# Score tiles without a clearing pass: the first unit on a tile multiplies with all keys of a block

## The chip, the cores and the metric

The kernel runs on one core of a Trainium2 chip. The metric is device time in microseconds of one execution; a kernel's time is the median over several executions. TensorE (PE in the profile, with PEld for its weight loads), VectorE (DVE), ScalarE (ACT), GpSimd (POOL) and SyncE (SP, which only issues DMAs here) each work through their own queue in order and wait for each other by semaphores.

## The reference

Sliding-window causal attention with a distance bias, followed by a feed-forward layer with the activation h * tanh(softplus(h)) (Mish). All inputs and outputs are float32.

```python
# attention: q, k, v are (8, 8, 576, 64); window = 128
scores = q @ k.T / 8 + slopes * (-abs(i - j))
mask = (i - j >= 0) & (i - j < 128)
attn = softmax(where(mask, scores, -1e9))          # / (sum + 1e-9)
x = (attn @ v).transpose(0, 2, 1, 3).reshape(4608, 512)
# feed-forward: w_in (512, 2048), w_out (2048, 512)
h = x @ w_in
out = (h * tanh(softplus(h))) @ w_out
```

## The kernel before

**Chunks and stages.** A chunk is the first 512 rows of one batch; the last 64 rows of all eight batches form a ninth chunk. The feed-forward layer works by chunk. Each float32 operand is split into a high and a low part, and a product is three matmuls (high x high, high x low, low x high). The program has a stage "first" (attention of batch 0, splitting of the weights, first layer of chunk 0) and stages 0 to 4. A stage holds the second layer of the chunks whose first layer is done (the step `second` in stages 0 and 1, `call` of `second_chain` in 2 and 3, of `second_fast` in 4), beside it the attention of the next chunks, and at its end the first layer of a pair of chunks as seven products (`product`), which share sums between the two chunks.

**A unit of attention.** `unit(b, p, half)` does two blocks of 128 queries for the two heads of pair p. Its steps are `scores` (PE), `peak` (VectorE: puts the older keys' scores over the newer block's where the window asks for it, adds the bias, takes the row's extreme), `exps` (ScalarE), `sums` (VectorE), `scale` (POOL), `weights` (PE transposes, then a VectorE product with the masks), `values` (PE), `split_hi` and `split_lo`. `last_unit` does the same for the 64 last rows.

**The score tile.** A score tile (`s`) is two PSUM banks: two heads, and per head two blocks of 256 columns, the older 128 keys and the newer 128. Two such buffers exist and take turns between score tiles, the products of the first layer (`h`, `m`) and others. Each half has a tile of its own, kept for all units of batch 0, and then for all units of a pair of chunks (1 and 2, 3 and 4, and so on). Queries 0 to 63 of a block need only keys 0 to 191 of the 256, queries 64 to 127 only keys 64 to 255; the first block of a batch has no older keys. So a call multiplies 64 queries with 192 keys (128 in the first block). The step `peak` reads the whole block with `copy_predicated`, also the corners that no call writes. Therefore `clear(b, half)` allocates the tile and writes zeros into the corners, two VectorE instructions per tile, ahead of the first unit; later units find finite numbers there.

**What sets the order.** Every step has a nominal time; `in_order` sorts a stage's steps by it, after the table `MOVED` has replaced some of the times by hand. Each engine executes its instructions in the order in which the sorted steps issue them. `idle` steps are filler matmuls in the stage "first" that write an unused tile. The steps carry no line of their own in the profile, since all instructions are issued by one helper (L82); tiles tell them apart: `s<-qk` are scores, `s<-ident,pz` transposes, `po` and `po_c` the second layer, `h` and `m` the first, `gs` and `gc` its split inputs, `pt_0l` last-row tiles, `so` and `si` split weights, `st` streamed weights.

Of the kernel before, what the change touches and what calls it, by code (L numbers as in the profile page):

```python
# [8 lines left out]
F32 = mybir.dt.float32  # L9
# [7 lines left out]
P = 128  # L17
# [1 line left out]

MOVED = {  # L20
    'first': {
# [7 lines left out]
    },  # L29
# [7 lines left out]
    },  # L37
# [9 lines left out]
    },  # L47
# [8 lines left out]
    },  # L56
# [6 lines left out]
    },  # L63
}

# [24 lines left out]
def attention_mish_mlp(  # L90
# [18 lines left out]
    H, D = 2 * NP, P // 2  # L109
# [17 lines left out]
    ps = ctx.enter_context(tc.tile_pool(name="ps", bufs=1, space=bass.MemoryType.PSUM))  # L127

    pe, dve, act, pool, sp = [
        InOrder(tc, e) for e in (nc.tensor, nc.vector, nc.scalar, nc.gpsimd, nc.sync)  # L130
    ]
# [109 lines left out]
    score = {}  # L241
    HEAD = [slice(i * D, (i + 1) * D) for i in range(2)]

    def clear(b, half):
        t = score[(b + 1) // 2, half] = ps.tile([P, 2, 512], F32, tag="s", name=f"s{b}_{half}", bufs=2)
        v = t.rearrange("p i (c u n) -> p (i c) u n", u=2, n=P)
        v = v if half else v[:, 1::2]
        dve.memset(v[HEAD[0], :, 1, D:], 0.0)
        dve.memset(v[HEAD[1], :, 0, :D], 0.0)

    def unit(b, p, half, turn=(0, 0), give=(0, 0), total=(0, 0), low=0, when=(0.9, 1.98, 2.04)):


# [6 lines left out]
        name = f"{b}_{p}_{half}"  # L260

        def scores():
            qk = qkv[(b, p)]
            key = ((b + 1) // 2, half)
            t = score[key]
            st["s"] = [t[:, i, :] for i in range(2)]
            st["all"] = t.rearrange("p i (c u n) -> p (i c) u n", u=2, n=P)
            q0 = 0 if half == 0 else 832
            for a, j in enumerate(blocks):
                for h in range(2):  # L270
                    k0, k1 = (D * h, D * h + 192) if j else (P, 2 * P)
                    for i in range(2):
                        pe.matmul(
                            st["s"][i][HEAD[h], 256 * a + k0 : 256 * a + k1],
                            lhsT=qk[HEAD[i], q0 + a * P + D * h : q0 + a * P + D * h + D],
                            rhs=qk[HEAD[i], 128 + j * P + k0 : 128 + j * P + k1], start=True, stop=True,
                            skip_group_check=True,
                        )
# [89 lines left out]
        t = half  # L368
# [84 lines left out]
    def loads(b, p):  # L453
        nxt = (b, p + 2) if p + 2 < NP else (b + 1, p + 2 - NP)
        if 0 < nxt[0] < B:
            return [lambda: load_qk(*nxt), lambda: load_v(*nxt)]
        return []

    def attention0():
        steps = [(-2 + 0.1 * h, lambda h=h: clear(0, h)) for h in range(2)]  # L460
        for p in range(NP):
            units = [(2 * p, unit(0, p, 0)), (2 * p, last_unit(0, p)), (2 * p + 1, unit(0, p, 1))]
            steps += [(k + d, f) for k, u in units for d, f in u]
            steps += [(2 * p + d, f) for d, f in zip((1.03, 3.01), loads(0, p))]
        return steps

    def attention(b, starts, form):

        steps = [(0.05 + 0.01 * h, lambda h=h: clear(b, h)) for h in range(2) if b % 2]
        for p in range(NP):
            k = starts[p]
            for u in (unit(b, p, 0, *form), last_unit(b, p, *form), unit(b, p, 1, *form)):
                steps += [(k + d, f) for d, f in u]
            steps += [(k + d, f) for d, f in zip((4.9, form[1][1] + 0.06), loads(b, p))]
        return steps
# [100 lines left out]
    steps = [(START + UNIT * t, f) for t, f in attention0()]  # L579
# [21 lines left out]
    for j in range(NJ):  # L601
        t = X0 + SLOT * j
# [500 lines left out]
    for s in range(len(PAIRS) + 1):  # L1103
# [7 lines left out]
        for o, c in enumerate(chunks):  # L1111
# [4 lines left out]
            for m in range(2 * NJ):  # L1116
# [4 lines left out]
                if s == 0 and m >= 2:  # L1121
                    t = PARTS[m - 2]
# [15 lines left out]
        if s < len(PAIRS):  # L1138
            a, b = PAIRS[s]
# [19 lines left out]
            for n in range(3):  # L1159
                t = (20, 30, 33) if s == 0 else (L - 7.5, L - 1.9, L + 0.1) if s >= FAST else (L - 7.5, L - 6.5, L - 5.5)  # L1160
# [13 lines left out]
            for k in range(len(PROD)):  # L1174
                n = 1 if s == 0 and k < 2 else 2
                for i in range(0, NF // 2, n):
# [4 lines left out]
                    for m in range((1, 2, 1, 2, 2, 3, 2)[k]):  # L1181
                        t = L + 8 * k + i + n + (0, 0.6, 2.5)[m] * (1 if m else 0)
                        if s == 0 and k < 2:
                            t = (t - 0.4, L + 24.6 + 0.8 * i)[m]
                        if m == 1 and k in (3, 5):
                            t = L + 8 * k + i + n + 0.1
                        put(t, lambda k=k, i=i, m=m: post[(k, i)][m][1]())
            nxt = split_fast if s + 1 == LAST else split_chain if s + 1 >= FAST else parts
            for n in range(2 if nxt is parts else 3):
                t = (51, 53) if nxt is parts else (50.7, 52.1, 53.2)  # L1190
# [96 lines left out]
```

## Time and profile before

| | us |
|---|---|
| median of 3 runs | 930.28 (927.7 to 930.71) |
| the profiled execution's own time | 927.47 |
| its span, first to last instruction | 925.8 |
| PE busy | 903.6 |
| VectorE busy | 654.0 |
| ScalarE busy | 469.3 |
| POOL busy | 430.5 |

Busy time is the union of an engine's instructions. Matmul ends are modelled, so a busy PE need not be at its peak. The stages of the profiled execution begin at about 88 us (stage 0), 254 (1), 458 (2), 661 (3) and 843 (4).

### The profile page before, as it was taken

To read this page: it belongs to the slowest core of one execution; us is meant where nothing else is said; L and a number is where in the kernel's file an instruction comes from. 1 tells how busy PE (TensorE), PEld (TensorE's weight loads), DVE (VectorE), ACT (ScalarE), POOL (GpSimd) and SP (SyncE) were. 2 spreads that over 40 slices of the span, in tenths; PEclk is the share of its full clock that TensorE was granted. 3 is DMA by queue.
4 is the path that set the end of the run, shared out by engine and by line. 5 is a ranking of instruction groups with operands and counts; after the bars stand their busy time and mean duration, and the time that the engine had idled before them with its cause. 6 is when DMAs were issued, how large, how long until landed. Compare 5 with 4: busy or idle time off the path is not lost.

```text
span 925.8 us, 17172 instructions
## 1 busy us (share of the span) xinstructions
PE 903.6 (98%) x6353; PEld 751.6 (81%) x6353; DVE 654.0 (71%) x1509; ACT 469.3 (51%) x1074; POOL 430.5 (47%) x316
## 2 busy tenths in 40 slices
PE   7998999999999999999999999999999999999998
PEld 3586777778778787888788999888799998888897
DVE  6989787685566677446688897545698645457986
ACT  5785655544464454352455646343555543336443
POOL 3202588714678877104667675014567670241000
PEclk9999999999999999999999999999999999999999
DMA  9999436798224444785426734855535367553823
GB/s 369 425 421 423 179 133 219 262 345 277 91 104 151 151 164 168 255 275 203 165 98 208 258 137 161 263 194 191 188 108 177 136 214 243 189 182 137 295 95 111
DMA packets 68291, 193.66 MB, mean 209 GB/s; under 512 B 10608, under 2 KB 14320, under 8 KB 64880
## 3 DMA queue, kind: packets, MB, share of 16 engines
q1 hardware_dynamic: 66544, 191.39, 58.2%
q10 hardware_dynamic: 1664, 1.18, 0.4%
q8 instruction: 50, 0.82, 0.4%
q14 instruction: 33, 0.27, 0.1%
HBM read 153.75 MB, written 38.80 MB: 208 GB/s over the span
## 4 chain that ended last, share of the span: by engine, by line
PE 80%; DVE 11%; ACT 4%; DMA 2%; POOL 2%; issue 2%; DVEq 0%; SPq 0%; POOLq 0%; ACTq 0%
PE m L82 31%; PE po L82 14%; PE po_c L82 13%; PE po_f L82 9%; PE s L82 6%; PE o L82 5%; DMA st<-wcS 2%; DVE to L82 2%; DVE pz L82 1%; ACT pz L82 1%; DVE ti L82 1%; POOL gc L82 1%; POOL pz L82 1%; DVE s L82 1%; DVE sm L82 1%
## 5 line engine op out<-in xcount | busy, mean ns | idle before, releaser
L82 PE MATMUL m<-xT,st 128*128 128x512 f32 x768 | 175.8, 389 | 0.4 <-DMA st<-wcS 0.4
L82 PEld LDWEIGHTS m<-xT,st 128*128 128x128 f32 x768 | 144.0, 188 | 30.9 <-issue 1.1
L82 PE MATMUL po<-so,gs 128*128 128x512 f32 x576 | 141.0, 398 | 0.0
L82 PE MATMUL m<-x,st 128*128 128x512 f32 x576 | 134.4, 391 | 0.0
L82 PEld LDWEIGHTS po<-so,gs 128*128 128x128 f32 x576 | 106.1, 189 | 25.8 <-issue 4.6
L82 PEld LDWEIGHTS m<-x,st 128*128 128x128 f32 x576 | 107.4, 188 | 23.2 <-ACT A L82 0.5
L82 ACT ACTIVATE pz<-pz,mx 128x128 f32<-128x128 f32 x256 | 99.5, 390 | 27.1 <-DVE mx L82 24.9
L82 POOL TENSOR_TENSOR D<-A,C 128x1024 f32<-128x1024 f32 x16 | 39.1, 2451 | 148.9 <-DVE A L82 84.6
L82 POOL TENSOR_TENSOR pz<-pz,sm 128x512 f32<-128x512 f32 x64 | 71.1, 1112 | 73.2 <-DVE sm L82 33.3
L82 PE MATMUL po_c<-so,gc 128*128 128x256 f32 x768 | 102.5, 289 | 1.8 <-POOL gc L82 1.8
L82 PEld LDWEIGHTS po_c<-so,gc 128*128 128x128 f32 x768 | 95.3, 192 | 7.4 <-issue 3.1
L82 DVE TENSOR_TENSOR pz<-s,masks 128x1024 f32<-128x1024 f32 x56 | 66.6, 1215 | 14.8 <-PE s L82 13.3
L82 PE MATMUL po_c<-sf,gc 128*128 128x256 f32 x576 | 73.4, 285 | 0.0
L82 PEld LDWEIGHTS po_c<-sf,gc 128*128 128x128 f32 x576 | 70.4, 191 | 1.7 <-issue 0.8
L82 DVE TENSOR_TENSOR A<-m,A 128x1024 f32<-128x1024 f32 x32 | 39.2, 1224 | 34.4 <-PE m L82 34.4
L82 POOL TENSOR_TENSOR C<-A,C 128x1024 f32<-128x1024 f32 x16 | 39.9, 2494 | 48.0 <-DVE A L82 36.2
L82 DVE CUSTOM_DVE_ANT_0 pz<-s,nb 128x128 f32<-128x128 f32 x256 | 59.2, 287 | 3.6
L82 PE MATMUL s<-qk 64*64 64x192 f32 (+1 forms) x1024 | 49.4, 324 | 10.3 <-DVE s L82 8.8
L82 DVE COPY_PREDICATED s<-older,s 128x256 f32<-128x256 uint16 x64 | 35.6, 556 | 25.7 <-PE s L82 25.5
L82 POOL TENSOR_TENSOR gc<-D,gc 128x512 fp32r<-128x512 f32 x28 | 39.1, 1415 | 28.8 <-ACT gc L82 26.6
L82 PEld LDWEIGHTS s<-qk 64*64 64x64 f32 x1024 | 32.8, 135 | 24.1 <-issue 18.1
L82 PE MATMUL o<-pz,va 128*64 128x128 f32 (+1 forms) x560 | 52.0, 320 | 0.0
(207 smaller groups left out, 1620.5 us busy)
## 6 DMA issues: line engine op xcount, KB each, us to landing
sf<-wdT SPq DMA_DIRECT2D x72, 512.0 KB, 4.5
st<-wcS SPq DMA_DIRECT2D x64, 512.0 KB, 4.7
st<-wr SPq DMA_DIRECT2D x48, 512.0 KB, 5.6
qk<-in_qk_dram SPq DMA_DIRECT2D x31, 640.0 KB, 5.9
va<-in_v_dram SPq DMA_DIRECT2D x28, 320.0 KB, 3.4
wi<-in_moe_w_in_dram SPq DMA_DIRECT2D x8, 1024.0 KB, 14.0
wo<-in_moe_w_out_dram SPq DMA_DIRECT2D x8, 1024.0 KB, 19.6
wr<-si SPq DMA_DIRECT2D x8, 1024.0 KB, 15.3
```

Source lines behind the costliest of these rows:

```text
L82: ins = method(*args, **kwargs)
```

## The change

The function `clear` and its steps go. The first unit on each tile (pair 0 of batch 0 and of chunks 1, 3, 5 and 7) allocates the tile in its own `scores` step and multiplies its queries with all 256 keys of a block, except in the first block of a batch, which still has 128. The other units are as before.

```diff
-    def clear(b, half):
-        t = score[(b + 1) // 2, half] = ps.tile([P, 2, 512], F32, tag="s", name=f"s{b}_{half}", bufs=2)
-        v = t.rearrange("p i (c u n) -> p (i c) u n", u=2, n=P)
-        v = v if half else v[:, 1::2]
-        dve.memset(v[HEAD[0], :, 1, D:], 0.0)
-        dve.memset(v[HEAD[1], :, 0, :D], 0.0)
...
             qk = qkv[(b, p)]
-            key = ((b + 1) // 2, half)
-            t = score[key]
+            full = p == 0 and (b == 0 or b % 2)
+            if full:
+                score[half] = ps.tile([P, 2, 512], F32, tag="s", name=f"s{b}_{half}", bufs=2)
+            t = score[half]
...
-                    k0, k1 = (D * h, D * h + 192) if j else (P, 2 * P)
+                    k0, k1 = (P, 2 * P) if not j else (0, 2 * P) if full else (D * h, D * h + 192)
...
-        steps = [(-2 + 0.1 * h, lambda h=h: clear(0, h)) for h in range(2)]
+        steps = []
...
-        steps = [(0.05 + 0.01 * h, lambda h=h: clear(b, h)) for h in range(2) if b % 2]
+        steps = []
```

The table `MOVED` is new for the stage "first" and stages 0 to 3 (the numbers of the steps shift by two where the clears were). On PE the steps at the start of each stage come in this order, with half 0 and half 1 for the scores of the first unit and "last" for those of the last rows:

```
stage 0 before: second(0,0), last, [clears] half 0, second(1,0), half 1, second(0,1), second(1,1)
stage 0 after:  half 0, second(0,0), second(0,1), half 1, last, second(1,0), second(1,1)
stage 1 before: last, [clears] half 0, half 1, second(0,0), second(0,1)
stage 1 after:  second(0,0), half 0, half 1, last, second(0,1)
stage 2 before: [clears] half 0, call 0, half 1, call 1, call 2, last
stage 2 after:  half 0, call 0, half 1, last, call 1, call 2
stage 3 before: [clears] half 0, call 0, call 1, half 1, last, call 2
stage 3 after:  half 0, call 0, half 1, call 1, call 2, last
```

Here second(j, t) is six matmuls with weight block j for row block t. In the stage "first" some 15 of 54 PE steps change place, `idle` fillers among them; after the first unit's scores six fillers now come ahead of the half-1 scores. Within stages 0, 1 and 3 `second` or `call` steps change places with transposes (`weights`) and `values`, last-row steps with main ones. On VectorE a few `weights`, last-row and split steps swap, in the stage "first" the words of weight block 2 come ahead of the low part of block 1; on ScalarE about eight steps move; on POOL two pairs swap; on SP the store of last rows with a load, and some stores of weight sums.

## Rows read from the trace of the kernel before

**Rows 1.** The page: busy us (share) of each engine, and the chain's shares.
```profile
PE 903.6 (98%) x6353; PEld 751.6 (81%) x6353; DVE 654.0 (71%) x1509; ACT 469.3 (51%) x1074; POOL 430.5 (47%) x316
...
PE 80%; DVE 11%; ACT 4%; DMA 2%; POOL 2%; issue 2%; DVEq 0%; SPq 0%; POOLq 0%; ACTq 0%
```

**Rows 2.** Waits of PE, whole span: who for whom, us, times, longest.
```profile
PE s L82 <- DVE s L82: 8.8, 4, 3.5
PE s L82 <- POOL pz L82: 2.8, 4, 1.5
PE po_c L82 <- POOL gc L82: 1.8, 6, 0.5
...
PE m L82 <- DMA st<-wcS: 0.4, 1, 0.4
```

**Rows 3.** Timeline at the start of stage 0: start us, us, engine, instruction [idle before].
```profile
83.16 1.01 ACT L82 ACTIVATE g<-h 128x1024 f32<-128x1024 f32 x1
...
85.68 1.52 PE L82 MATMUL po<-so,gs 128*128 128x512 f32 x6
...
87.38 1.01 ACT L82 ACTIVATE g<-h 128x1024 f32<-128x1024 f32 x1
88.16 2.43 DVE L82 TENSOR_TENSOR so<-to,so 128x1024 fp32r<-128x1024 f32 x2
...
90.61 1.22 DVE L82 MEMSET s<- 64x128 f32 x4
...
91.19 0.78 PE L82 MATMUL s<-qk 64*64 64x128 f32 x16 [3.51 <-DVE s L82]
...
92.02 0.43 DVE L82 COPY_PREDICATED s<-older,s 128x256 f32<-128x256 uint16 x1 [0.19 <-PE s L82]
...
92.94 1.28 ACT L82 ACT_TABLE_LOAD   x1 [3.08 <-DVE mx L82]
...
94.04 1.56 PE L82 MATMUL s<-qk 64*64 64x192 f32 x16
94.23 0.40 ACT L82 ACTIVATE pz<-pz,mx 128x128 f32<-128x128 f32 x1
...
97.86 1.04 POOL L82 TENSOR_TENSOR pz<-pz,sm 128x512 f32<-128x512 f32 x1 [6.14 <-DVE pt_0l L82]
...
100.05 0.60 PE L82 MATMUL s<-ident,pz 128*128 128x128 f32 x4
```

**Rows 4.** Windows: stretch, length, busy PE, PEld, DVE, ACT, POOL, clock, DMA, GB/s.
```profile
91.00:97.00 6.00, 5.81 (x43) 3.76 (x44) 3.25 (x18) 3.15 (x10) 0.71 (x1) 0.72 1.02 417
460.00:466.00 6.00, 5.75 (x53) 4.62 (x54) 2.92 (x16) 3.10 (x6) 1.28 (x1) 0.72 0.84 334
660.00:668.00 8.00, 6.08 (x65) 4.65 (x64) 4.55 (x16) 3.53 (x5) 2.87 (x3) 1.00 0.73 263
5.00:42.00 37.00, 31.69 (x322) 17.91 (x320) 32.14 (x127) 26.13 (x88) 10.69 (x12) 1.00 1.02 422
42.00:85.00 43.00, 43.00 (x189) 35.21 (x188) 39.34 (x38) 32.14 (x33) 3.73 (x2) 1.00 1.02 423
```

**Rows 5.** Timelines at the starts of stages 1, 2 and 3.
```profile
251.18 1.22 DVE L82 TENSOR_TENSOR A<-A,m 128x1024 f32<-128x1024 f32 x1 [1.50 <-PE m L82]
253.90 1.22 DVE L82 TENSOR_TENSOR A<-A,m 128x1024 f32<-128x1024 f32 x1 [1.50 <-PE m L82]
...
255.71 1.67 PE L82 MATMUL s<-qk 64*64 64x128 f32 x32 [1.45 <-DVE s L82]
...
458.43 1.22 DVE L82 TENSOR_TENSOR A<-A,m 128x1024 f32<-128x1024 f32 x1 [1.50 <-PE m L82]
...
460.25 0.77 PE L82 MATMUL s<-qk 64*64 64x128 f32 x16 [1.93 <-DVE s L82]
...
662.77 0.78 PE L82 MATMUL s<-qk 64*64 64x128 f32 x16 [1.92 <-DVE s L82]
...
666.53 0.88 PE L82 MATMUL s<-qk 64*64 64x192 f32 x16
```

68 rows, old and new, of the table MOVED are left out of this document.

## The prediction

> **What bounds the kernel now.** I read the page's busy shares first, then the chain that ended last: TensorE (PE) is busy for 903.6 of 925.8 us and carries 80% of the chain [rows 1]. So only what makes PE wait, or makes it slower, is worth anything, and the next view is who PE waited for [rows 2]. One entry stands out: four waits of 8.8 us in total, longest 3.5 us, of a score multiplication (`s`) on VectorE (DVE) work on the same score tile. PE and DVE meet on `s` in that direction at the clears, and there are four starts of stages 0 to 3 where a pair of tiles is cleared. I then went to each of the four in the order of time.
>
> At the first, near 88 us, PE has little to do from the end of its six `po` matmuls (85.68 + 1.52 = 87.2) until 91.19; VectorE is in the two subtractions `so` from 88.16 and reaches the clears only at 90.61 [rows 3]. The tile itself was free much earlier: its former content `h` was read at 83.16 to 84.17. So the wait is not for the tile but for a VectorE queue in which the clear stands last. The other three look alike: the last `A` operation (at 253.90, and at 458.43 for stage 2) reads the *other* score buffer; the buffer that the first unit gets was read by the `A` before it (251.18 + 1.22 = 252.4); and the clears stand behind the last one. PE idles 1.45, 1.93 and 1.92 us [rows 5].
>
> The windows add a second cost. From 91 to 97 us and from 460 to 466 us the granted clock averages 0.72 of full speed, so 0.28 x 6 = 1.7 us of full-speed work is lost in each, right behind the idle 3.51 and 1.93 us [rows 4]. The fourth, with 1.92 us, shows 1.00 from 660 to 668. The 16 matmuls of a half-1 unit tell the same: 1.56 us at 94.04, 0.88 at 666.53 [rows 3, 5].
>
> **The change part by part.**
>
> *Wider first units, five times (batch 0 and chunks 1, 3, 5, 7).* Per unit every call is two instructions. A half-0 unit has 8 instructions with 128 columns and 8 with 192 (0.78 us, at 662.77), a half-1 unit 16 with 192 (0.88 us, at 666.53) [rows 5]. So 64 columns more on 8 instructions cost 0.10 us. The change widens 8 instructions of half 0 and 16 of half 1: 0.30 us of PE per start. The wide shape is in no row; from below the cost is 0 (hidden in an idle PE, as for batch 0, where PE waits anyway), from above it is 0.6 us, if such a unit runs at half clock. I take 0.30 at four starts, 0 at batch 0. On this the Trainium skill, "TensorEngine Tiling", section "Tiling Modes", says that the 64x64 mode has four independent tiles. The rows don't bear that out: 8 x 64 = 512 columns in 0.10 us is about two columns at a time at 2.4 GHz, not four. By that section of the Trainium skill the cost would be an estimated 0.15 us per start and the time 0.6 us lower.
>
> *Twenty clears go.* Four take 1.22 us of VectorE per start [rows 3]; what it is worth is the waits. I also have to say what is late next, since the new order changes what PE does there.
>
> *Start of stage 0.* New PE order: half-0 scores, two `second` steps of 6 matmuls, half-1 scores, last scores, three more `second` steps, then the transposes of the first weights. PE is free for them at 85.7 [rows 3]. Half 0 takes 0.88, so 86.6; two steps at 1.52 or a little less each (row at 85.68) 89.6; half 1 needs the last `h` read at 87.38 + 1.01 = 88.4, is not held, and ends at 90.7; the last-row scores are smaller than a half-0 unit, under 0.78; three steps, 96.0 at the latest. The other side starts from VectorE, still in `so` until 90.6. It begins `peak` there and not at 92.02, so 1.4 us earlier; the table load follows 0.92 us behind (92.94 - 92.02), at 91.5; the exponentials 1.29 us later, at 92.8; four at 0.40, 94.4; sums of 0.4 us; GpSimd's scale of 1.04 us; transposes at about 96.0. Before, they began at 100.05 [rows 3]. PE waits there for 0 to 1.5 us, and 4.0 us are won: 3.5 of idle and 1.7 of clock, less 0.3 for the columns and what the new wait takes. What waits behind the head of PE's queue, if a score step is held, is all `second` steps, and behind those the slots for the next `gs`.
>
> *Start of stage 1.* The new order puts one `second` step ahead of the scores, and its operands were ready. Idle 1.45 less 0.30: 1.15 us.
> *Start of stage 2.* Same order as before, with the scores at the head; their buffer was left by the `A` before the last, as at 251.18. 1.93 + 1.7 of clock - 0.3 = 3.3 us.
> *Start of stage 3.* Half-1 scores move ahead of the second `call`; the other buffer is free when the last `A` ends, 0.6 us ahead of the old scores (459.65 against 460.25 at stage 2), so at about 662.2, before PE gets there. 1.92 - 0.30 = 1.6 us.
> Bounds of these four together: 0 from below, if each wait finds another name; from above 8.8 + 3.4 - 1.2 = 11.0.
>
> *The refit of stage "first".* About 15 PE steps move, fillers (`idle`) among them. From 42 to 85 us PE is busy 43.00 of 43.00 us, so whatever is won or lost before 42 reaches the boundary. From 5 to 42 VectorE is busy 32.14 of 37 us [rows 4], so at most 4.9 us can be won; I see moves both ways (second-half scores of pair 1 earlier; the last-row `peak` and a split placed ahead of half-1 work, later), and the split of weight block 1 now stands behind 1.9 us of block 2's words. I take 0.3 won, bounds 2 lost and 4.9 won.
>
> *Other moves.* Elsewhere `second` steps swap with transposes, and last-row steps with main ones. On POOL two pairs swap, on SP an `xs` store with a load and some stores of weight sums. No PE wait hangs on these: all PE waits on POOL work are 4.6 us, on DMA `st` 0.4 [rows 2]. I take 0, bounds 2 either way.
>
> *What is late next.* PE comes to later steps 4 to 10 us earlier than its partners were used to. Most of these follow PE, but not all; I take off 0.8, bounds 0 and 4.3.
>
> **Sum.** 4.0 + 1.15 + 3.3 + 1.6 + 0.3 - 0.8 = 9.55 us. The profiled execution took 927.47 us (1.67 of it outside its span), so 917.9, say 918. The median of the three runs is 930.28, 2.8 us above that execution. As a start of 1.93 us idle lost its clock and one of 1.92 did not, I read the 2.8 as one or two more such losses of 1.7; without idle they go too. Against the median I therefore forecast 12 us less.
>
> **The rivals.**
> *The first gain is given back.* At 207 us PE waits 0.4 us for `st`, loaded behind the combined weights that POOL and the DMAs make [rows 2]. If that chain does not follow PE, the 4.0 us (and the 0.3) end there as a wait for `st`: 922.2. For it: it is already the last to arrive. Against: 0.4 us only, and POOL idles in between.
> *The wait changes its name.* If the first unit's buffer is the one read last, PE waits for that reader. Stage 0: scores at 88.4 rather than 91.19, with the idle and clock loss kept, so some 1 us won; stage 1 is covered by the step put ahead, 1.15; at stages 2 and 3 `A` ends at 459.65 against 460.25, 0.6 - 0.3 each. About 2.8 won: 924.7. Against: two buffers take turns, and 83.16 and 251.18 are the reads of the other one.
> *The refit wins more.* PE's waits on POOL (4.6 us) and half of stage first's idle VectorE (2.4) go in part: 3.5 us beyond the forecast, 914.4.
> *Slower: the clock falls in stage first.* From 5 to 42 us PE's 31.69 busy us [rows 4] hold fillers that keep it occupied between waits of up to 1.5 us, and the refit moves them. At half clock that work takes 31.7 us more against 5.3 of idle: up to 26 us lost, and with 9.3 won elsewhere some 944. It decides once about 15 of the 31.7 us run at half. Against: the row's clock is 1.00 with the same number of fillers.
>
> **How the numbers follow.** Forecast 0.57; first gain given back 0.18; the refit wins more 0.12; the wait renamed 0.08; slower by the clock 0.03; no net effect for several small reasons 0.02. The forecast's own range is 915.5 to 921. From 914 to 923 the range takes in the first three and their spread, about 0.82. A measurement can tell about 0.3%, 2.8 us: faster than 927.5 are the first four, 0.93 with their tails off; 0.04 within, 0.03 slower.
>
> **What would show it.** No row of PE waiting on DVE for `s` at stage starts; granted clock 1.00 at 91 to 97 and 460 to 466; score units of 0.88 and 1.08 us in first units; transposes of chunk 1's first unit near 96; the product stage of chunk 2 beginning about 9 us earlier by 843. It is wrong if PE has a wait of over 3 us near 207, if the products of stage first start later than 41.7, or if PE idles at the four starts under another name.

## The result and the profile after

The kernel after takes 919.6 us in the median (919.28 to 920.5, 4 runs) against 930.42 for the kernel before on the same chip (927.7 to 930.71, 4 runs): a ratio of 0.9892 [0.9872, 0.9912]. The profiled executions compare 919.29 with 927.47, that is 8.2 us less; 918.0 (914 to 923) was forecast.

The waits of PE over the whole span (who for whom, us, times, longest), which answer to [rows 2]:

```profile
PE s L84 <- POOL pz L84: 3.5, 4, 1.4
PE po_c L84 <- POOL gc L84: 1.5, 6, 0.4
PE idle L84 <- DVE busy L84: 1.3, 1, 1.3
PE pt_2l L84 <- DVE pz_2l L84: 1.0, 1, 1.0
PE pt_1l L84 <- DVE pz_1l L84: 0.8, 1, 0.8
PE pt_3l L84 <- DVE pf_3l L84: 0.8, 1, 0.8
PE pt_0l L84 <- DVE pz_0l L84: 0.7, 1, 0.7
PE o L84 <- DVE pf L84: 0.7, 1, 0.7
PE m L84 <- DMA st<-wcS: 0.7, 1, 0.7
```

The entry of 8.8 us, `s` on VectorE's `s`, is gone. What is new stands lower down: PE's last-row transposes (`pt_1l`, `pt_2l`) wait for VectorE's last-row scale (`pz_1l`, `pz_2l`), and `st` has grown from 0.4 to 0.7. The windows answer to [rows 4]; the third and fourth hold the starts of stages 2 and 3, which now come earlier:

```profile
5.00:42.00 37.00, 31.75 (x324) 18.14 (x321) 32.48 (x126) 26.12 (x88) 10.99 (x12) 1.00 1.02 422
91.00:97.00 6.00, 5.33 (x28) 4.08 (x25) 3.97 (x28) 5.50 (x20) 2.32 (x3) 1.00 1.01 412
455.00:461.00 6.00, 6.00 (x66) 4.69 (x66) 4.72 (x20) 4.49 (x11) 1.45 (x2) 1.00 0.85 307
650.00:660.00 10.00, 10.00 (x79) 7.84 (x78) 7.25 (x22) 7.45 (x12) 5.46 (x4) 1.00 0.66 240
```

The clock (last but two) is 1.00 in all of them, and PE is busy throughout the starts of stages 2 and 3. The timeline at the start of stage 0 answers to [rows 3]:

```profile
85.86 0.88 PE L84 MATMUL s<-qk 64*64 64x128 f32 x16
86.67 3.01 PE L84 MATMUL po<-so,gs 128*128 128x512 f32 x12
...
88.22 2.44 DVE L84 TENSOR_TENSOR so<-to,so 128x1024 fp32r<-128x1024 f32 x2
89.61 1.09 PE L84 MATMUL s<-qk 64*64 64x256 f32 x16
90.58 0.42 DVE L84 COPY_PREDICATED s<-older,s 128x256 f32<-128x256 uint16 x1
...
91.49 1.28 ACT L84 ACT_TABLE_LOAD   x1 [1.57 <-DVE mx L84]
...
95.08 1.04 POOL L84 TENSOR_TENSOR pz<-pz,sm 128x512 f32<-128x512 f32 x1 [3.27 <-DVE pt_0l L84]
...
96.17 0.66 PE L84 MATMUL s<-ident,pz 128*128 128x128 f32 x4 [0.67 <-POOL pz L84]
...
98.08 1.27 DVE L84 TENSOR_SCALAR pz_0l<-pz_0l,sm_0l 128x128 f32<-128x128 f32 x1
...
99.40 0.33 PE L84 MATMUL pt_0l<-ident,pz_0l 128*128 128x128 f32 x1 [0.74 <-DVE pz_0l L84]
```

Scores run while VectorE is still in the two `so` subtractions; the peak begins when these end (90.58 instead of 92.02), and the transposes start at 96.17 instead of 100.05, 3.9 us earlier. The last two rows show the price: VectorE's last-row scale comes behind a mask product, and PE waits 0.74 us for it (0.61 before, at 103.09).

**Where the time went.** The same matmul of both profiles, start after minus start before, followed through the span:

| at | behind or ahead, us | change in the stretch | forecast |
|---|---|---|---|
| first VectorE peak (5.16 before, 5.52 after) | +0.36 | | |
| end of stage "first" | +0.09 | 0.27 won | 0.3 won |
| first transposes of stage 0 | -3.88 | 3.97 won | 4.0 won |
| end of stage 0's beginning (130 us) | -2.07 | 1.81 lost | |
| start of stage 1 | -1.87 | 0.20 lost (`st`) | |
| start of stage 2 | -3.31 | 1.44 won | 1.15 won |
| 470 us, peak of stage 2 | -6.69 | 3.38 won | 3.3 won |
| start of stage 3 | -5.77 | 0.92 lost | |
| end | -8.19 | 2.42 won | 1.6 won |

The three losses, 2.93 us, stand against the 0.8 that was set for "what is late next".

### The profile page after: what moved, and what is told of

Read it like the earlier page. It is cut to its first block, busy times and chain, and to the rows that moved or that the text cites. A ratio compares the mean times of both kernels' runs of the same rounds, so it can differ in the third digit from the quotient of the medians.

```text
span 917.6 us, 17138 instructions
## 1 busy us (share of the span) xinstructions
PE 901.8 (98%) x6349; PEld 749.9 (82%) x6353; DVE 655.8 (71%) x1489; ACT 468.8 (51%) x1074; POOL 433.1 (47%) x316
## 5 line engine op out<-in xcount | busy, mean ns | idle before, releaser
L84 PE MATMUL s<-qk 64*64 64x192 f32 (+2 forms) x1024 | 49.1, 324 | 0.5 <-DVE pf L84 0.5
L84 ACT ACTIVATION_READ_ACCUMULATOR pz<-pz,mx 128x1 f32 x256 | 48.1, 188 | 0.0
```

The lines of the kernel that those rows point to most:

```text
L84: ins = method(*args, **kwargs)
```

## The experiments

Each kernel was run beside the kernel before; ratios are to that. Runs 1 to 4, 5 to 7, 8 and 9, and 10 to 12 are four sets, each on a chip of its own, where the kernel before took 928.81, 929.19, 927.9 and 930.17 us. Of the table `MOVED` the diffs from run 6 on print the changed entries only. The theory: the cost of a clear is its place in VectorE's queue, ahead of which PE could have gone on; with it go the half-speed stretches that follow PE's idle. The rivals: the refit of the order carries the gain; the clears cost by their own work; the half-speed stretches have another cause; the first gain is held by something later.

**1. No clears, old order.** The kernel after with the old times of `MOVED`, two indices lower behind the clears.

```diff
     0: {
-        8: 8.5, 12: 8.6, 17: 9.11, 21: 14.2, 26: 14.4, 34: 17.1,
...
+        0: -13.2, 1: 3.1, 2: -12.8, 3: 3.8, 8: 8.5, 9: 8.3, 12: 9.11,
...
```

> The kernel after with the old written order (each index behind the clears lowered by two): no clears and wide first units, no refit. Theory A (the clears' place in VectorE's queue was the cause, the refit is trimming): no PE wait for s on VectorE at the four starts, granted clock 1.00 throughout, 919 to 922 us, that is within 2 us of the kernel after. Theory B (the refit carries a good part, because the old order was fitted around the clears): waits under other names at the starts, 923 to 926 us.

919.42 us (918.78 to 920.61, 4 runs), ratio 0.9906 [0.9893, 0.992]; no PE wait for `s` on VectorE, clock 1.00. Theory A: the removal alone brings what the whole change brings. In the traces, each counted from its own first peak, this kernel won 7.7 us and the kernel after 8.5, the difference mostly in stages 1 and 3; in the medians no difference is seen.

**2. Clears kept, but earlier in VectorE's queue.** The kernel before with five clears moved.

```diff
+        def clear_here(h):
+            if (b, h) not in ((1, 0), (1, 1), (3, 0), (5, 0), (7, 0)):
+                clear(b, h)
...
+    steps += [(84.0, lambda: clear(1, 0)), (89.0, lambda: clear(1, 1))]
     for f in in_order(steps, "first"):
...
+        if s < 3:
+            put((87, 119, 111)[s], clear, 2 * s + 3, 0)
         for f in in_order(work, s):
```

> The kernel before with its clears kept and five of them moved on VectorE: the clear of half 0 goes ahead of the last A (stages 1 to 3) or ahead of the two so subtractions (stage 0, half 1 between them); columns and order of everything else as before. Theory A (place in the queue): the four waits of 8.8 us shrink to under 2 us in sum and the clock stays at 1.00 in both stretches, but VectorE still spends 1.22 us per start, of which the start of stage 0 passes on about 1.2 us: 920 to 923 us. Rival (the clears cost by the work they put on VectorE, or PE would wait for the previous content anyway): 926 us or more.

921.72 us (920.97 to 921.91), ratio 0.9928 [0.9915, 0.994]. PE at the start of stage 2, and the waits:

```profile
452.77 4.47 PE L82 MATMUL m<-xT,st 128*128 128x512 f32 x19
457.17 0.77 PE L82 MATMUL s<-qk 64*64 64x128 f32 x16
457.88 1.69 PE L82 MATMUL po_c<-so,gc 128*128 128x256 f32 x12
```

```profile
PE s L82 <- DVE s L82: 1.8, 2, 1.1
```

The half-0 scores follow the last product with no idle, with the clear still there: it runs on VectorE ahead of the last `A`. 7.1 us (928.81 - 921.72) are won by place alone, with every clear still executed; the kernel after won 9.5 in run 7 (929.19 - 919.72). Against run 1 this kernel lacks 2.3 us in the medians and 1.2 in the traces: 1.3 at the start of stage 0 and 0.7 in stage 1, less 0.6 at `st`. At these two starts the half-1 scores still wait for their clears, 0.75 us at 91.45 and 1.09 at 255.43.

**3. The new order alone.** The kernel before with the new `MOVED` (indices raised by two behind the clears), clears at the head of each stage.

```diff
     0: {
+        8: 8.5, 12: 8.6, 17: 9.11, 21: 14.2, 26: 14.4, 34: 17.1,
...
+        128: -1000.0, 129: -999.0, 130: -15.3, 136: 5.6, 143: 4.96,
...
```

> The kernel before with the new written order alone: clears kept, at the head of VectorE's work of each stage as before, 192 columns. Theory A: the waits for s on VectorE stay at over 7 us in sum, and 927 to 932 us, no gain (at stage 0 the score step now stands ahead of all second steps, so it may lose 1 to 2 us). Theory B (the refit carries a good part): 922 to 926 us.

929.3 us (927.56 to 930.46, 11 runs), ratio 1.001 [1.0, 1.0019]: nothing. At stage 0 the score step, which the new order puts ahead of all `second` steps, holds PE's queue for 5.38 us, and the clock falls. PE there, and the windows at the starts of stages 0, 2 and 3:

```profile
83.76 2.88 PE L84 MATMUL h<-x,si 128*128 128x512 f32 x12
92.02 1.34 PE L84 MATMUL s<-qk 64*64 64x128 f32 x16 [5.38 <-issue]
```

```profile
91.00:97.00 6.00, 4.98 (x28) 3.70 (x28) 2.71 (x14) 2.65 (x8) 1.60 (x1) 0.62 1.02 419
460.00:466.00 6.00, 4.08 (x51) 2.76 (x50) 3.91 (x15) 2.34 (x4) 1.03 (x2) 1.00 0.76 277
660.00:668.00 8.00, 6.08 (x53) 4.50 (x52) 4.67 (x16) 3.14 (x4) 2.50 (x3) 0.85 0.70 254
```

The profile names no releaser ("issue"), but VectorE begins the clears at 91.49 us, behind the same two `so` subtractions, and the scores start at 92.02. Runs 1 to 3 settle the first rival: without the refit all is won, with the refit alone nothing.

**4. Keep PE busy while it waits.**

```diff
+    def fill(n):
+        t = ps.tile([P, 512], F32, tag="o", name="fill")
+        for _ in range(n):
+            pe.matmul(t, lhsT=masks[:, 0, :], rhs=nb[:, 0].rearrange("p h n -> p (h n)"), start=True, stop=True)
...
+        if s in (0, 2):
+            put(-12.95 if s == 0 else -4.35, fill, 15 if s == 0 else 8)
```

> The kernel before with matmuls of 512 columns that nobody reads put ahead of the first scores at two starts, 15 at stage 0 and 8 at stage 2 (some 3.2 and 1.7 us): PE is kept busy while it waits for the clear, the wait itself stays. Theory A (the half-speed stretches of 3.41 us follow from the idle): granted clock 1.00 from 91 to 97 and from 460 to 466, half-1 scores of stage 0 in 0.9 us instead of 1.56, and up to 3.4 us won, of which 0.7 to 1.5 may be given back in stage 0: 924 to 926 us. Rival (the clock falls for another reason, or the lost speed was hidden behind VectorE): no change, 927 to 931 us.

927.19 us (925.5 to 929.53, 11 runs), ratio 0.9983 [0.997, 0.9996]. The two windows, and PE at the start of stage 0:

```profile
91.00:97.00 6.00, 5.87 (x51) 3.82 (x50) 4.33 (x25) 3.35 (x12) 1.42 (x1) 1.00 1.01 414
460.00:466.00 6.00, 5.82 (x63) 4.41 (x62) 4.34 (x22) 3.35 (x5) 1.30 (x1) 1.00 0.93 345
```

```profile
88.34 3.41 PE L82 MATMUL fill<-nb,masks 128*128 128x512 bf16 x15
91.89 0.77 PE L82 MATMUL s<-qk 64*64 64x128 f32 x16
92.59 1.66 PE L82 MATMUL po<-so,gs 128*128 128x512 f32 x6
94.18 0.88 PE L82 MATMUL s<-qk 64*64 64x192 f32 x16
```

The clock is 1.00 where it was 0.72, and the half-1 scores take 0.88 us instead of 1.56 [rows 3]: the half-speed stretches do follow from the idle. At the two places 2.3 and 1.5 us are won; but 1.15 us go again in stage 0's last rows, 1.4 at a wait of 1.89 us for `st` near 205, and 0.6 in stage 2. In this trace 0.7 of the 3.8 us are left, in the median 1.6. The 924 to 926 expected were not reached: theory A had the cause, and not the amount that stays.

**5. All score units wide.**

```diff
-  k0, k1 = (P, 2 * P) if not j else (0, 2 * P) if full else (D * h, D * h + 192)
+  k0, k1 = (P, 2 * P) if not j else (0, 2 * P)
```

> The kernel after with 256 columns in every score unit instead of the first on each tile: 27 more pairs of units. Theory A (TensorE is the bound and two 64-row products run at a time, so 0.107 us per half-0 unit and 0.213 per half-1 unit, 0.32 per pair): 27 x 0.32 = 8.6 us at most, 7.7 without the three pairs of batch 0; 926.5 to 928.5 us. Rival (four at a time, or the columns hide in waits of PE): half of it or less, under 924 us.

926.42 us (925.98 to 928.02, 11 runs), ratio 0.9974 [0.9965, 0.9982]; the kernel after, run beside it, took 919.72. So 6.7 us for 27 pairs, 0.25 per pair. In the trace the three pairs of batch 0 cost 0.92 us together (0.31 each), the other 24 cost 5.7 (0.24 each): part of the columns fall into waits. The rival (half or less) is out; A's 926.5 to 928.5 was missed by 0.1 us.

**6. The last-row scales first.** Stage 0's give-back, tried on the kernel after.

```diff
     0: {
-        141: 4.96, 153: 9.06,
+        141: 4.12, 153: 9.105, 196: 13.98, 197: 13.99, 204: 13.97,
...
```

> The kernel after with VectorE's order changed at three places of stage 0: the last-row scale of pair 0 ahead of the mask of half 0, of pair 1 (with its sums) ahead of the split of x, of pair 2 (with both sums) ahead of the copy of ob. Theory A (what stage 0 gave back, 1.7 us net of its first gain, is these waits of PE on pz_0l, pz_1l, pz_2l: 0.74 + 0.77 + 1.05 = 2.56 us): the three waits fall under 0.3 us each, and 1.5 to 2.5 us are won if the wait for st near 204 does not take it: 917 to 918.5 us. Rival (the stretch is bound by the chain of VectorE and GpSimd behind it, or st takes it): the waits move to pz, pf or st, under 0.6 us won: 919 to 920 us.

918.64 us (917.89 to 920.24), ratio 0.9886 [0.9873, 0.9899]. Two of the three waits went; the third doubled, and `st` took its share:

```profile
PE m L84 <- DMA st<-wcS: 1.8, 1, 1.8
PE pt_1l L84 <- DVE pz_1l L84: 1.6, 1, 1.6
```

1.1 us less than the kernel after beside it, where the runs of the two overlap (917.89 to 920.24 against 919.35 to 921.12); short of A's 1.5 to 2.5, and the expected end of all three waits is refuted: at `pt_1l` PE now comes still earlier than VectorE, which spends 3.8 us on the bit operations of a weight block ahead of pair 1's sums. In the trace 1.0 us was won by 128 us, and `st` took it back: all of it against the first profile of the kernel after, 0.6 us against that of run 7. The median of the five runs (918.64) lies below the profiled one (920.24).

**7. The kernel after once more.**

> The kernel after, unchanged, beside the two others. 919 to 920.5 us. It tells how much executions of one kernel differ by the work ahead of the first VectorE step (5.16 us in the profile before, 5.52 after, 5.9 to 6.0 in the four experiments so far).

919.72 us (919.35 to 921.12), ratio 0.9901 [0.9888, 0.9913]. Its first VectorE peak stands at 6.11 us, 0.6 later than in the first profile, and its waits for `st` are 1.2 us instead of 0.67: an unchanged kernel differs by this much between executions, and single profiles tell nothing below about 1 us of the end.

**8 and 9. Load `st` earlier by moving work to GpSimd**, with run 6's edit (8) and without (9).

```diff
-            e = dve if j == 3 else pool
-            e.tensor_tensor(out=w[:, 1, k].bitcast(F32R), in0=w[:, 1, k], in1=w[:, 0, k], op=ALU.subtract)
+            pool.tensor_tensor(out=w[:, 1, k].bitcast(F32R), in0=w[:, 1, k], in1=w[:, 0, k], op=ALU.subtract)
...
     0: {
+        122: 43.5, 123: 43.51, 124: 44.0, 367: 44.01,
...
```

> The kernel with the last-row scales first (as in the run of that name), and besides, in stage 0, the four subtractions that make the low parts of the last combined weight block go from VectorE to GpSimd (idle from 188.7 to 212.7 us in the profile after), the first two of them right behind ScalarE's high parts, and their store and the load of st with them: some 3 us earlier (192.4 against 195.4). Theory A (the wait for st near 204, 0.67 to 1.8 us in the runs so far, takes back what stage 0 won): the wait goes, 1.0 to 1.8 us less than with the scales alone: 916.5 to 917.8 us. Rival (the landing of st hangs on the DMA queues, not on its issue; or PE then waits for B or C there): 918.2 to 919.5 us.

> The kernel after with only the second of these edits (low parts on GpSimd, store and load of st earlier). Theory A: the wait for st, 0.67 to 1.2 us in the two profiles of the kernel after, goes: 918.4 to 919.2 us. Rival as above: 919.3 to 920.5 us.

920.01 us (919.76 to 920.4), ratio 0.9907 [0.9889, 0.9924], and 921.63 (920.45 to 921.97), ratio 0.9921 [0.9903, 0.9939]: in the medians 1.4 us above run 6 and 1.9 above run 7, each on another chip and with ratios whose intervals overlap. No gain, so theory A is refuted. The wait for `st` did go, but PE waits 2.1 and 2.2 us for VectorE's `B`: the rival's second reason, at a price above its range and for a cause that it did not name. VectorE and GpSimd in run 9, and VectorE in the kernel after:

```profile
190.54 6.36 POOL L84 TENSOR_TENSOR cw<-cw 128x512 fp32r<-128x512 f32 x4 [1.17 <-ACT cw L84]
190.85 0.68 DVE L84 TENSOR_TENSOR B<-m,A 128x512 f32<-128x512 f32 x1
...
192.41 1.67 DVE L84 TENSOR_TENSOR T<-T,x 128x512 f32<-128x512 f32 x1
194.01 0.68 DVE L84 TENSOR_TENSOR B<-m,A 128x512 f32<-128x512 f32 x1
194.61 2.84 DVE L84 TENSOR_TENSOR xT<-T,xT 128x512 fp32r<-128x512 f32 x2
```

```profile
191.49 0.69 DVE L84 TENSOR_TENSOR T<-T,x 128x512 f32<-128x512 f32 x1
192.29 0.69 DVE L84 TENSOR_TENSOR B<-m,A 128x512 f32<-128x512 f32 x1
192.89 1.28 DVE L84 TENSOR_TENSOR xT<-T,xT 128x512 fp32r<-128x512 f32 x2
```

While GpSimd subtracts, two of VectorE's steps whose inputs both lie in SBUF take more than twice as long (0.69 to 1.67, 1.28 to 2.84), and those that read `m` from PSUM do not (0.69 and 0.68). The Trainium skill, "SBUF — State Buffer", section "SBUF: two separate sides", says that VectorE operations with two SBUF inputs and GpSimd's share a port pair that one of them holds for a whole instruction; these rows agree with it.

**10 and 11. Less traffic ahead of `st`**, with run 6's edit (10) and without (11). The next batch's `qk` and `va` (nominal times 42.9 and 43.22) go behind the loads of `st`.

```diff
     0: {
+        351: 47.2, 352: 47.21,
...
```

> The kernel with the last-row scales first, and besides the last two loads of the next batch's qk and va in stage 0 (640 and 320 KB, issued at 186.5 and 190.7 us in the profile after) put behind the loads of st that PE waits for near 204. The DMA engines are busy for 1.01 to 1.05 of 180 to 195 us and 0.93 to 0.96 of 195 to 207, so these 0.96 MB at some 350 GB/s stand some 2.7 us ahead of st. Theory A (the wait for st is the DMA engines' backlog): the wait (1.8 us with the scales alone) falls under 0.3 us, 1.2 to 1.6 us less than with the scales alone (918.6): 917.0 to 917.5 us. Rival (the landing hangs on the store of wcS and its own latency): wait of 1 us or more, 918.2 to 919 us.

> The kernel after with only the two loads moved. Theory A: the wait for st (0.67 and 1.2 us in its two profiles) goes: 918.7 to 919.2 us. Rival: no change, 919.3 to 920.5 us.

918.12 us (917.06 to 918.24, 4 runs), ratio 0.9869 [0.9847, 0.9891], and 919.13 (918.7 to 920.35, 6 runs), ratio 0.9884 [0.9865, 0.9904]. The wait for `st` is gone from both profiles, and the two transfers that end it are shorter, as theory A's cause has it: the store of `wcS` took 3.71 us to land in the kernel after and 2.72 in both runs, the load of `st` behind it 6.08 us, then 5.00 and 5.24. The window from 180 to 195 us, first of the kernel after, then of run 10 (the last but one column is the DMA engines' busy share):

```profile
180.00:195.00 15.00, 15.00 (x102) 11.74 (x95) 13.78 (x43) 7.89 (x25) 6.55 (x6) 1.00 1.05 376
```

```profile
180.00:195.00 15.00, 15.00 (x95) 11.76 (x88) 13.81 (x44) 7.81 (x24) 6.20 (x6) 1.00 0.93 334
```

The engines were full ahead of `st` (1.05) and are less so now (0.93, and 0.99 in run 11). In time run 11 met A's 918.7 to 919.2; run 10 missed A's 917.0 to 917.5 by 0.6 us and is 0.5 below run 6, a difference that these two medians can't prove. Run 10 has the lowest median, and its four runs lie below all those of the kernel after, which were taken on other chips.

**12. Also the bit operations later.** As run 10, with the two bit operations (and the high part behind them) put behind pair 1's last-row peak.

```diff
     0: {
-        65: 7.1,
+        65: 8.35, 66: 8.45,
...
```

> As the first of these three, and VectorE's two bit operations of the last weight block (some 3.7 us while GpSimd works beside them) with ScalarE's high part behind them put behind the last-row peak of pair 1 instead of ahead of its sums, so that the wait for pz_1l (1.6 us) falls to under 0.4 us. Theory A (that wait is the queue ahead of it on VectorE): another 0.8 to 1.3 us: 916.0 to 916.6 us. Rival (what moves behind it is late for the weight block, and PE waits there): 917 to 918.5 us.

918.21 us (917.53 to 918.84), ratio 0.9873 [0.9851, 0.9894]: no gain over run 10. The wait for `pz_1l` fell only from 1.6 to 1.2 us, and VectorE's queue still makes it:

```profile
108.77 0.69 DVE L85 TENSOR_SCALAR to<-wo 128x1024 uint32<-128x1024 uint32 x1
109.49 1.23 DVE L85 SCALAR_TENSOR_TENSOR to<-wo,to 128x1024 uint32<-128x1024 uint32 x1
110.63 0.16 DVE L85 TENSOR_SCALAR sm<-sm 128x4 f32<-128x4 f32 x1
...
111.28 1.02 DVE L85 TENSOR_SCALAR pz_1l<-pz_1l,sm_1l 128x128 f32<-128x128 f32 x1
```

The moved operations now stand ahead of the next sums, whose exponentials ScalarE had ended at 109.50, so these begin 1.1 us late; the scale then takes 1.02 us beside GpSimd. Theory A's size is refuted for this edit; its cause was not taken away.

## Why the prediction was right, step by step

**What bounds it, and the cause: shown.** Run 2 wins 7.1 us with every clear kept and only its place changed, run 1 all of it without the refit, run 3 nothing without the removal.

**Start of stage 0: the steps came in the order and nearly at the times forecast** (half 0 to 86.7 for 86.6, half 1 to 90.7, peak 90.6, table load 91.5, transposes 96.17 for "about 96.0"), 3.97 us for 4.0.

**What is late next: the term that failed in size**, 2.9 us lost for 0.8. Of it 1.81 us went within 34 us of the first gain, at three waits of PE for VectorE's last-row scale (0.74, 0.77 and 1.05 us; 0.61, 0 and 0.26 before); the one place that I had named was `st` at 207 us. The rival "the first gain is given back" was thus half right in effect (2.0 of 4.0 us) and had the place wrong: `st` took 0.2 us in the first profile, though 0.9 in run 7 and 1.4 in run 4. Runs 6 and 10 show the two causes by taking parts of them away. The places won more than forecast, 11.5 us for 10.35, so the total (8.5 from the first VectorE peak, for 9.55) is closer than its terms; that they offset is luck.

**Stage 2: 3.38 us won at the place for 3.3**, of which 0.92 went again: 0.63 between 474 and 476 (before's times) and 0.26 at 535, in front of matmuls that read `gc`. That `gc`, split by ScalarE and GpSimd, did not follow PE is read from the trace and was not tried.

**Stages 1 and 3 won more than forecast** (1.44 for 1.15, 2.42 for 1.6). In run 1, without the refit, they won 1.12 and 1.91: the idle was closed as forecast, and the rest comes with the new order; in stage 3, two waits of PE for `gc` of 0.34 us each shrank to one of 0.24. The refit is thus worth up to 0.8 us in single traces, and nothing that the medians show.

**The wide columns: the price right, the reason wrong.** A half-0 unit takes 0.88 for 0.78 us, a half-1 unit 1.09 for 0.88, which is 0.31 per start for the 0.30 taken. Batch 0 was put at 0; run 5 puts a wide pair at 0.31 there too. I read this as two tiles at a time at one column per cycle. The starts in the trace of the kernel after say otherwise: the first four of the 16 instructions at 89.61 start within 0.02 us, and the last two groups of four 0.216 us behind the one before, that is 256 columns in some 518 cycles at 2.4 GHz (granted clock 1.00). So four run at once, at two cycles per column; the transposes of `pz` on the whole array, float32 too, take as long (128 columns, 0.109 us from start to start). The Trainium skill, "TensorEngine Tiling (Array Packing)", section "Tiling Modes", lists four tiles for 64x64, and the trace agrees; my estimate of half the price went by one cycle per column. In run 5's expectation the theory's "two at a time" is wrong in the same way; its price per pair stands.

**Stage "first": 0.27 for 0.3**, but from one profile; in run 3, with the same order, it is -0.07. It is within what executions of one kernel differ.

**The clock: the cause shown (run 4), and the reading of the median borne out in kind.** I took the 2.8 us between the median before and its profiled execution for further half-speed stretches. Every execution has its mean granted clock beside its time. Over the 59 executions of the kernel before in the four sets of experiments the time goes with it:

| mean granted clock | executions | median, us |
|---|---|---|
| 0.998 | 18 | 927.7 |
| 0.996 | 11 | 928.8 |
| 0.994 | 18 | 929.8 |
| 0.992 | 5 | 931.9 |

Seven more have clocks between these. The profile before has 0.996 and loses some 0.28 x 6 = 1.7 us of full-speed work at each of two places [rows 4]; 1.7 of 926 us is 0.0018, so the table's rows stand for some one to four such places (an estimate from these figures), at 1.0 to 2.1 us each. The profiled execution itself (927.47) lies 1.3 us below the median at its clock, so a part of the 2.8 us is something else. Run 4's spread follows the clock too: 928.67 and 929.53 us at 0.997, 925.5 to 928.21 at 0.999 and 1.00. The kernel after shows 0.999 or 1.00 in all nine executions; against the median it won 10.8 us of the 12 forecast. What decides how many such places an execution has stays open. The kernel before has a median of 928.81 over 21 executions in the first set of experiments, so the gain by medians is 9 to 11 us.

## What to carry to other kernels

A small operation that another engine waits for costs by what stands ahead of it in its queue, not by its duration: first ask whether it can go earlier (run 2: 7.1 of 9.5 us with no other edit), then whether it can go. When a stall is removed, list the next operations of the stalled engine and who feeds them within the next tens of us, for that is where a quarter of the gain was given back here (2.9 of 11.5 us). Take idle in front of matmuls at more than its length, but book only part of the clock's return.

## What the runs showed of the hardware

- Half speed followed an idle PE, and filling the idle kept full speed (run 4); but an idle of 1.92 or 1.93 us was followed by a clock below 1 at the start of stage 2 in the profile before and of stage 3 in run 3, and by 1.00 at stage 3 before and stage 2 in run 3 [rows 4]. Which of them falls was not settled; the executions of the kernel before differ in it (table above).
- GpSimd beside VectorE made VectorE steps with both inputs in SBUF up to 2.4 times as long (0.69 to 1.67 us, run 9). In the kernel after, the last-row scale of 128x128 took 1.27 us at 98.08, where it ended 0.08 us after GpSimd's split of `gs` (97.99 to 99.27), and 0.26 at 173.20, where none of GpSimd's tensor operations ran. In the kernel before it took 1.14 us at the first of these places, so its length is for the most part not what the change made late.
- A score instruction of 64 rows and 64 columns on float32 took two cycles per column at 2.4 GHz, and four of them ran at once (kernel after, from 89.61).
- With the DMA engines at a share of 1.05 from 180 to 195 us, the 512 KB of `st` that PE waited for landed 6.08 us after their issue in the kernel after; with 0.96 MB taken from ahead of them 5.00 and 5.24 us (runs 10 and 11), and PE no longer waited.
